# Batch 1 of a block-recurrent attention + ELU kernel: its turns taken from TensorE to VectorE and transfers, its state reading moved into its own first product

## The chip, the cores and the metric

The kernel runs on one core of one Trainium2 chip. The metric is device time in microseconds (us) for one execution. Below, PE is TensorE (matrix products), DVE is VectorE, ACT is ScalarE, POOL is GpSimd, and SP is the engine whose queue issues nearly all transfers.

## The reference

```python
B, H, S, Ns, D = 8, 8, 512, 32, 64             # x: (B,H,S,D), state: (B,H,Ns,D)
scale = 1.0 / np.sqrt(D)
scores = scale * np.matmul(x, state.transpose(0, 1, 3, 2))
a = np.exp(scores - scores.max(-1, keepdims=True))
a /= a.sum(-1, keepdims=True) + 1e-09
xread = np.matmul(a, state)                    # tokens read the state
scores2 = scale * np.matmul(state, x.transpose(0, 1, 3, 2))
a2 = np.exp(scores2 - scores2.max(-1, keepdims=True))
a2 /= a2.sum(-1, keepdims=True) + 1e-09
sread = np.matmul(a2, x)                       # the state reads the tokens
attn = np.concatenate([xread, sread], axis=2)
x = attn.transpose(0, 2, 1, 3).reshape(B * (S + Ns), H * D)
h = x @ w_in                                   # 512 -> 2048
g = np.where(h > 0.0, h, np.exp(np.minimum(h, 0.0)) - 1.0)
return (g @ w_out).astype(np.float32)          # 2048 -> 512
```

The weights come as 8-byte floats and are brought to 4 bytes in the kernel.

## The kernel before, in words

The work goes batch by batch over the eight batches, and the 256 state rows of all batches (what the state read) come last (`states`). For one batch there are these parts:

- **Attention.** `scores` multiplies the state with x, which has to stand with its features on the partitions, so x has to be *turned* first. There are two ways in the kernel. `turn_x` (L251) turns it on TensorE, 16 small products with the identity for each half of x, into PSUM, and `copy_x` (L260) copies it out with ScalarE. `load_blocks` (L141) and `turn_blocks` (L159) read x from memory in 16 transfers that already put the 32x32 blocks in place, and VectorE turns each block in itself, one instruction of 128x512 for a quarter of x. Then come the maxima, exponentials and sums (`column_max`, `column_exp`, `row_max`, `row_subtract` and so on), for two groups of heads g.
- **The state's reading.** `state_read` (L374) multiplies the column weights with x as loaded. For it the weights have to be turned: `turn_state` and `copy_state` (L347, L354) do it on TensorE and ScalarE, `move_state` (L359) with two block turns on VectorE and 16 transfers that put the blocks in place (`a_blocks` to `aT_s`). `keep_read` (L390) scales the result out of PSUM with ScalarE.
- **First product.** `make_m` (L418) multiplies the state into w_in, into a pair of PSUM banks, `copy_m` copies it to `m_sb`; `ffn1(b, fo)` (L453) makes one of 16 slices `fo` of the hidden layer from `m_sb` and the turned token weights `aT`. `exp_part` (ACT) and `max_part` (DVE) are the ELU and write `g_all`.
- **Second product.** In the first batch it is the plain one (`ffn2_row`, L480). From batch 1 on it is Strassen's scheme (class `Strassen`), partly in two levels (`Second`): its `sums()` (L589) are four VectorE instructions on `g_all`, two into `g_all` and two into `s`; its steps are seven products, the first in several pieces, and between the pieces the "hooks" of the next batch's attention run.

Batch 0, the batch in which all weights are also loaded and brought to 4 bytes, follows an order written out by hand: the string `plan` (L747). It also makes the attention of batch 1. In a step `name:numbers`, `w:n.1` and `w:n.2` are the two halves of bringing weight piece n to 4 bytes (ACT, DVE), `F`, `R`, `E`, `O` are the first product, exponential, maximum and output row of a slice, `M` and `Mc` make and copy m, `x` and `xc` are `turn_x` and `copy_x`, `sc` the scores, `mx tr ae sd tm ps te su pm tt` the steps of the softmax by group, `sT sTc sr src` turn, copy, reading and keeping of the state. Each `w:n.2` calls `fetch()`, which loads the next piece; when none is left it loads x of batch 1 and stores w_in for later.

The engines are wrapped in `InOrder` (L94): while `on` is set, each instruction is pinned behind everything that was traced before it on its engine. Otherwise a scheduler at compile time orders each engine's instructions by when its own model has them ready, earlier ones of the program first. TensorE and SP are pinned to the end. ScalarE and GpSimd are let go after the first batch, and VectorE in `batch(1)` (L864), and it stays so for the rest:

```python
        vector.on = False
        nxt = b + 1 < B
        hooks = attention(b + 1) if nxt else [turn_read]
```

In `batch(b)` (L847) the loop over `fo` makes the 16 slices. At `fo == 5` it calls `make_m` for the second half of w_in, in the last four slices it turns the blocks of the next batch, and in batch 1 every odd slice also makes a part of the weight sums (`weight_sum`) for Strassen's scheme, the last of them into `w_out`. After the loop come the sums and the steps. `hooks` holds for the next batch: scores to `move_state` behind the first piece, `state_read` and `keep_read` behind the seventh, then `load_x(b + 2)`, and in batch 1 the weights of `Second`.

Space: x as loaded (`x_sb`) has one buffer. The tiles of `tag="o"` (turned x, x in blocks, outputs) have two, those of `tag="w"` (weights as loaded, `xT_b`, `aT_s`, `a_blocks`, `t_w`, `s`) eleven. PSUM has eight banks; `pair(6)` is banks 6 and 7.

Of the kernel before, what the change touches and what calls it, by code (L numbers as in the profile page):

```python
# [25 lines left out]
def kernel(  # L26
# [106 lines left out]
    def load_x(b, engines):  # L133
        x_t[b] = xpool.tile([P, R, DM], FP32, name="x_sb")
        x_v = x[b].rearrange("h (p r) d -> p r h d", r=R)
        for r in range(R):
            engines[r % len(engines)].dma_start(
                out=x_t[b][:, r].rearrange("p (h d) -> p h d", d=D), in_=x_v[:, r]
            )
# [111 lines left out]
    def turn_x(b, i, first=6):  # L251

        ps = pair(first).rearrange("p t (j r q) -> p t j r q", j=2, q=64)
        for j in range(2):
            for r in range(R):
                m = 2 * i + j
                transpose(ps[:, :, j, r], x_t[b][:, r, m * P : (m + 1) * P])
        st[b, "xT", i] = ps
# [480 lines left out]
    def first_batch():  # L739

        plan = """  # L747
            kT kTc x:0.0 xc:0.0 x:0.1 w:0.1 xc:0.1 w:0.2 w:1.1 sc:0 Z:14 tr:0.0 tr:0.1 w:2.1 tm:0.0
            tm:0.1 ps:0.0 w:3.1 mx:0.1 mx:0.0 ps:0.1 w:1.2 ae:0.0 te:0.1 ae:0.1 sd:0.0 su:0.1 w:5.1
            M:0.0.0 sd:0.1 pm:0.1 w:3.2 Mc:0.0.0 te:0.0 sT:0 w:4.1 tt:0.1 su:0.0 sTc:0 w:5.2 pm:0.0  # L750
            w:8.1 Z:8 sr:0 tt:0.0 src:0 w:2.2 Z:14 F:0 w:6.1 F:1 w:8.2 R:0 M:0.0.1 R:1 E:0 Mc:0.0.1
            E:1 O:0 w:9.1 w:4.2 w:10.1 w:9.2 F:2 w:7.1 w:6.2 M:0.1.0 F:3 R:2 w:7.2 Mc:0.1.0 O:1
            w:11.1 E:2 R:3 w:10.2 M:0.1.1 w:12.1 F:4 w:11.2 Mc:0.1.1 O:2 R:4 E:3 w:14.1 w:12.2 F:5
            w:13.1 E:4 w:14.2 O:3 R:5 w:16.1 E:5 w:13.2 F:6 w:17.1 w:16.2 M:0.2.0 R:6 F:7 w:18.1
            w:17.2 O:4 Mc:0.2.0 w:18.2 w:20.1 kU w:15.1 E:6 O:5 w:20.2 w:21.1 w:15.2 w:19.1 F:8 kUc
            O:6 R:8 w:21.2 R:7 w:22.1 E:7 M:0.2.1 E:8 F:9 w:19.2 Mc:0.2.1 w:23.1 M:0.3.0 F:10 w:22.2
            w:24.1 O:7 w:23.2 R:9 Mc:0.3.0 E:9 w:25.1 w:24.2 M:0.3.1 F:11 Mc:0.3.1 R:10 w:25.2 O:8
            R:11 E:10 w:26.1 E:11 F:12 w:29.1 w:26.2 O:9 w:30.1 w:29.2 w:27.1 F:13 w:30.2 w:28.1
            O:10 w:27.2 R:13 R:12 w:28.2 x:1.0 w:31.1 O:11 E:12 E:13 xc:1.0 w:31.2 x:1.1 O:12 xc:1.1
            sc:1 O:13 mx:1.1 mx:1.0 ae:1.1 tr:1.0 ae:1.0 tr:1.1 sd:1.0 sT:1 tm:1.0 tm:1.1 ps:1.0  # L760
            F:14 sTc:1 sd:1.1 ps:1.1 te:1.0 sr:1 R:14 su:1.0 F:15 te:1.1 pm:1.0 E:14 src:1 su:1.1
            O:14 R:15 tt:1.0 pm:1.1 E:15 tt:1.1 M:1.0 O:15 Mc:1.0
        """.split()
        make_identity(nc, ident)
        o_ps = [bank(c) for c in range(R)]
        order = [lambda k=k: load_w_in(0, k) for k in range(4)]
        for c in range(1, FC + 1):
            if c < FC:
                order += [lambda c=c, k=k: load_w_in(c, k) for k in range(4)]
            order += [lambda fo=fo: load_w_out(fo) for fo in range(4 * c - 4, 4 * c)]  # L770
        w, h, e = [], {}, {}

        def fetch():
            if len(w) == 12 and len(raw_states) == 1:
                raw_states.append(load_states(1, B))
            if len(w) < len(order):
                w.append(order[len(w)]())
            elif 1 not in x_t:
                load_x(1, [sync])
                for c in range(FC):  # L780
                    k = slice(2 * c, 2 * c + 2)
                    sync.dma_start(out=w_in_mem[:, k], in_=w_in[:, k])

        raw_states = [load_states(0, 1, [sync, scalar])]
        load_x(0, [sync, scalar])
        for k in range(NRAW):
            fetch()
        groups = {
            "mx": column_max, "tr": turn_scores, "ae": column_exp, "tm": row_max,
            "ps": row_subtract, "te": row_exp, "su": row_sum, "pm": row_scale,  # L790
            "tt": turn_tokens, "sd": column_total,
        }
        whole = {
            "sc": scores, "sT": turn_state, "sTc": copy_state, "sr": state_read,
            "src": keep_read,
        }
        for step in plan:
            name, _, num = step.partition(":")
            num = [int(i) for i in num.split(".") if i]
            if name in ("kT", "kU"):  # L800
                turn_states(raw_states[name == "kU"], *((0, 1) if name == "kT" else (1, B)))
            elif name in ("kTc", "kUc"):
                copy_states(*((0, 1) if name == "kTc" else (1, B)))
            elif name == "Z":
                for i in range(num[0]):
                    matmul(bank(3)[:, :P], ident, ident, start=True, stop=True)
            elif name in groups:
                groups[name](*num)
            elif name in whole:
                whole[name](*num)  # L810
            elif name == "w":
                (convert_1, convert_2)[num[1] - 1](*w[num[0]])
                if num[1] == 2:
                    fetch()
            elif name == "F":
                h[num[0]] = ffn1(0, num[0])
            elif name == "R":
                e[num[0]] = exp_part(h[num[0]])
            elif name == "E":
                max_part(num[0], e[num[0]], h[num[0]])  # L820
            elif name == "O":
                ffn2_row(o_ps, num[0])
            elif name == "x":
                turn_x(*num)
            elif name == "M":
                make_m(*num)
                if len(num) == 2:
                    make_m(1, 1, first=4)
            elif name == "xc":
                copy_x(*num)  # L830
            else:
                assert name == "Mc", step
                if len(num) == 3:
                    copy_half(*num)
                else:
                    for g in range(G):
                        copy_m(*num, g, scalar.copy)
        for g in range(G):
            copy_m(1, 1, g, scalar.copy)

        for i in (1, 0):
            o_sb = opool.tile([P, 2, DM], FP32, tag="o", name="o_sb")
            for c in (1, 0):
                (scalar.copy, vector.tensor_copy)[c](out=o_sb[:, c], in_=o_ps[2 * i + c])
            store(0, i, o_sb)

    def batch(b):  # L847
        if b + 1 < B:
            load_blocks(b + 1)
        for fo in range(FO):  # L850
            elu(ffn1(b, fo), fo)
            if fo > 11 and b + 1 < B:
                turn_blocks(b + 1, fo - 12)
            if fo == FO // 4 + 1:
                for c in (2, 3):
                    make_m(b, c, first=6 if c == 2 else 0)
            if FO // 4 + 1 <= fo < FO // 4 + 5:
                c, g = divmod(fo - FO // 4 - 1, G)
                copy_m(b, 2 + c, g, vector.tensor_copy)
            if b == 1 and fo % 2 == 1:  # L860
                weight_sum((1, 2, 4, 3)[fo // 4], fo % 4 // 2)
            if b > 1 and fo == FO // 4 + 2:
                fetch_w_in(0, 0)
        vector.on = False  # L864
        nxt = b + 1 < B
        hooks = attention(b + 1) if nxt else [turn_read]
        if nxt and b > 0:
            s1 = hooks[0]
            hooks[0] = lambda: (s1(), fetch_w_in(2, 0))
        if b + 2 < B:  # L870
            hooks += [lambda: load_x(b + 2, [sync])]
        if b == 1:
            hooks += [lambda: second[4].weights(t_w[4]), lambda: second[3].weights(b22)]
            hooks += [lambda: second[5].weights(t_w[1]), lambda: second[7].weights(t_w[3])]
            used = {k: second[k] for k in (4, 3)}
        else:
            used = second
        whole = Strassen(2, used)
        whole.sums()
        for f in whole.steps():  # L880
            f()
            if hooks:
                hooks.pop(0)()
        if not nxt:
            fetch_w_in(2, 2)
        for i in (1, 0):
            store(b, i, whole.o_sb[i])
# [22 lines left out]
                )  # L910

    first_batch()
    load_x(2, [sync])
    for e in (scalar, gpsimd):
        e.on = False
    for b in range(1, B):
# [32 lines left out]
```

## Time and profile before

| | us |
|---|---|
| three runs | 746.68, 748.34, 748.26; median 748.26 |
| profiled execution, its own time | 746.17 |
| its span in the profile | 744.4 |

| place in the span | us |
|---|---|
| scores of batch 1 (TensorE) | 109.68 to 110.70 |
| first slice of batch 1 | from 128.72 |
| `make_m` of batch 1's second half | 139.11 to 140.99 |
| end of batch 1's first product | 159.29 |
| scores and `make_m` for batch 2 | 162.83 to 168.93 |
| reading of batch 2 | from 189.84 |

The granted TensorE clock is 1.0 throughout. In the lists of instructions the columns are start and length in us, engine, operation, what is written and read, and how many were put together in the row; in square brackets stands how long the engine was idle before, and what ended it. Products overlap on TensorE: the length of one row reaches into the next, so the price of a row is the step from its start to the start of the next one. The same holds for VectorE on a smaller scale. All instructions go through a wrapper, so all bear its line, L100, and are told apart by their tiles. A product of 4-byte floats is recorded as two.

### The profile page before, as it was taken

To read this page: it belongs to the slowest core of one execution; us is meant where nothing else is said; L and a number is where in the kernel's file an instruction comes from. 1 tells how busy PE (TensorE), PEld (TensorE's weight loads), DVE (VectorE), ACT (ScalarE), POOL (GpSimd) and SP (SyncE) were. 2 spreads that over 40 slices of the span, in tenths; PEclk is the share of its full clock that TensorE was granted. 3 is DMA by queue.
4 is the path that set the end of the run, shared out by engine and by line. 5 is a ranking of instruction groups with operands and counts; after the bars stand their busy time and mean duration, and the time that the engine had idled before them with its cause. 6 is when DMAs were issued, how large, how long until landed. Compare 5 with 4: busy or idle time off the path is not lost.

```text
span 744.4 us, 11377 instructions
## 1 busy us (share of the span) xinstructions
PE 723.7 (97%) x4472; PEld 502.5 (68%) x4472; DVE 486.0 (65%) x892; ACT 293.3 (39%) x539; POOL 34.4 (5%) x38
## 2 busy tenths in 40 slices
PE   4899999989999999999999999999999999999998
PEld 2544444348874798469944896479746894699886
DVE  2999975799437883677556864787367845556231
ACT  5899955542126311651055203621264106400420
POOL 0100002002000200010000200020002000000000
PEclk9999999999999999999999999999999999999999
DMA  9667900801634063503461164307340403003000
GB/s 282 225 201 239 326 0 1 167 4 22 177 94 133 5 179 84 160 1 106 122 153 46 26 173 110 116 13 187 83 144 1 143 33 137 1 1 142 29 4 25
DMA packets 126366, 76.25 MB, mean 102 GB/s; under 512 B 113768, under 2 KB 114280, under 8 KB 122472
## 3 DMA queue, kind: packets, MB, share of 16 engines
q1 hardware_dynamic: 124004, 74.90, 34.8%
q10 hardware_dynamic: 2308, 0.62, 0.4%
q8 instruction: 35, 0.57, 0.3%
q14 instruction: 19, 0.16, 0.1%
HBM read 59.24 MB, written 13.11 MB: 97 GB/s over the span
## 4 chain that ended last, share of the span: by engine, by line
PE 89%; DVE 6%; SPq 1%; DMA 1%; ACT 1%; issue 1%; POOL 0%; ACTq 0%; DVEq 0%; POOLq 0%
PE ps L100 89%; DVE w_in L100 2%; SPq L100 1%; DMA x_sb<-in_x_dram 1%; DVE g_all L100 1%; DVE total_t L100 0%; DVE s L100 0%; DVE top L100 0%; DVE w_out L100 0%; ACT e_sb L100 0%; POOL t_sb L100 0%; ACT xT L100 0%; DVE xT_b L100 0%; DVE aT L100 0%; DVE t_sb L100 0%
## 5 line engine op out<-in xcount | busy, mean ns | idle before, releaser
L100 PE MATMUL ps<-w_out,g_all 128*128 128x256 f32 (+2 forms) x1088 | 232.5, 366 | 1.1 <-DVE g_all L100 0.8
L100 PE MATMUL ps<-aT,m_sb 128*128 128x512 f32 x512 | 226.3, 595 | 1.1 <-DVE m_sb L100 0.8
L100 PEld LDWEIGHTS ps<-w_out,g_all 128*128 128x128 f32 x1088 | 176.6, 191 | 53.5 <-issue 37.1
L100 PEld LDWEIGHTS ps<-aT,m_sb 128*128 128x128 f32 x512 | 95.4, 190 | 122.0 <-issue 109.1
L100 ACT ACTIVATE e_sb<-ps 128x512 f32<-128x512 f32 (+1 forms) x144 | 82.5, 573 | 220.4 <-PE ps L100 205.1
L100 DVE SCALAR_TENSOR_TENSOR g_all<-e_sb,ps 128x512 f32<-128x512 f32 (+1 forms) x144 | 94.2, 656 | 101.0 <-ACT e_sb L100 100.4
L100 DVE TENSOR_TENSOR o_sb<-o_sb,ps 128x128 f32<-128x128 f32 (+2 forms) x170 | 52.6, 310 | 75.2 <-PE ps L100 73.5
L100 ACT ACTIVATE e_sb<-e_sb 128x512 f32<-128x512 f32 (+1 forms) x144 | 87.3, 606 | 4.6
L100 PE MATMUL ps<-t_w,s 128*128 128x256 f32 (+1 forms) x480 | 88.8, 339 | 0.0
L100 PEld LDWEIGHTS ps<-t_w,s 128*128 128x128 f32 x480 | 77.6, 191 | 8.1 <-DVE o_sb L100 0.2
L100 ACT COPY o_sb<-ps 128x512 f32<-128x512 f32 (+2 forms) x52 | 20.6, 424 | 151.7 <-PE ps L100 144.6
L100 ACT ACTIVATE raw<-raw 128x512 f32<-128x512 uint32 x64 | 43.7, 683 | 1.0
L100 DVE TENSOR_TENSOR s<-s,g_all 128x512 f32<-128x512 f32 (+1 forms) x36 | 32.2, 897 | 15.9 <-PE ps L100 15.5
L100 POOL TENSOR_TENSOR t_sb<-t_sb,top_t 128x512 f32<-128x512 f32 x16 | 16.7, 1047 | 517.0 <-DVE top_t L100 517.0
L100 DVE TENSOR_TENSOR g_all<-g_all,s 128x512 f32<-128x512 f32 (+1 forms) x36 | 32.1, 891 | 9.6 <-PE ps L100 9.6
L100 PE MATMUL ps<-w_in,kT 64*32 64x512 f32 (+1 forms) x576 | 34.0, 547 | 0.9 <-ACT a_s L100 0.9
L100 DVE TENSOR_TENSOR g_all<-g_all 128x512 f32<-128x512 f32 (+1 forms) x36 | 32.2, 894 | 0.5
L100 DVE TENSOR_TENSOR s<-g_all 128x512 f32<-128x512 f32 (+1 forms) x36 | 31.6, 883 | 0.8 <-DMA aT_s<-a_blocks 0.4
L100 PE MATMUL ps<-t_w,g_all 128*128 128x128 f32 (+1 forms) x240 | 32.1, 282 | 0.0
L100 PE MATMUL ps<-w_in,s 128*128 128x128 f32 x240 | 31.2, 277 | 0.0
L100 PEld LDWEIGHTS ps<-t_w,g_all 128*128 128x128 f32 x240 | 29.8, 192 | 0.5
L100 PEld LDWEIGHTS ps<-w_in,s 128*128 128x128 f32 x240 | 28.7, 192 | 0.6 <-DVE o_sb L100 0.5
(86 smaller groups left out, 557.1 us busy)
## 6 DMA issues: line engine op xcount, KB each, us to landing
w_in<-w_in_mem SPq DMA_DIRECT2D x26, 1024.0 KB, 5.9
raw<-in_moe_w_in_dram SPq DMA_DIRECT2D x16, 512.0 KB, 4.6
raw<-in_moe_w_out_dram SPq DMA_DIRECT2D x16, 512.0 KB, 4.5
out_dram<-o_sb SPq DMA_DIRECT2D x16, 512.0 KB, 2.8
x_sb<-in_x_dram SPq DMA_DIRECT2D x30, 256.0 KB, 4.9
x_blocks<-in_x_dram SPq DMA_DIRECT2D x96, 64.0 KB, 2.4
w_in_mem<-w_in SPq DMA_DIRECT2D x4, 1024.0 KB, 8.3
aT_s<-a_blocks SPq DMA_DIRECT2D x96, 32.0 KB, 1.9
```

What stands on the lines that cost most here:

```text
L100: ins = getattr(self.engine, name)(*args, **kw)
```

## The change

In `plan`, the steps `x xc` and `sT sTc sr src` of batch 1 are taken out. In place of the first come four `bt` (`turn_blocks`), in place of the second comes `ab` (`move_state`), on VectorE between the row sum and the maximum of slice 14. `fetch()` loads x in blocks ahead of x as it is. The reading of batch 1 is made at `fo == 5` of `batch(1)`, and the load of batch 2's x, which needs x's one buffer, moves behind it. The two pairs of banks of `make_m` there are exchanged for batch 1. And VectorE is let go behind `whole.sums()` rather than ahead of the hooks, so that the four sums of batch 1 stay in the order of the program.

```diff
--- before.py
+++ after.py
@@ -756,9 +756,9 @@
             O:6 R:8 w:21.2 R:7 w:22.1 E:7 M:0.2.1 E:8 F:9 w:19.2 Mc:0.2.1 w:23.1 M:0.3.0 F:10 w:22.2
             w:24.1 O:7 w:23.2 R:9 Mc:0.3.0 E:9 w:25.1 w:24.2 M:0.3.1 F:11 Mc:0.3.1 R:10 w:25.2 O:8
             R:11 E:10 w:26.1 E:11 F:12 w:29.1 w:26.2 O:9 w:30.1 w:29.2 w:27.1 F:13 w:30.2 w:28.1
-            O:10 w:27.2 R:13 R:12 w:28.2 x:1.0 w:31.1 O:11 E:12 E:13 xc:1.0 w:31.2 x:1.1 O:12 xc:1.1
-            sc:1 O:13 mx:1.1 mx:1.0 ae:1.1 tr:1.0 ae:1.0 tr:1.1 sd:1.0 sT:1 tm:1.0 tm:1.1 ps:1.0
-            F:14 sTc:1 sd:1.1 ps:1.1 te:1.0 sr:1 R:14 su:1.0 F:15 te:1.1 pm:1.0 E:14 src:1 su:1.1
+            O:10 w:27.2 R:13 R:12 w:28.2 w:31.1 bt:1.0 bt:1.1 O:11 E:12 bt:1.2 E:13 bt:1.3 w:31.2 O:12
+            sc:1 O:13 mx:1.1 mx:1.0 ae:1.1 tr:1.0 ae:1.0 tr:1.1 sd:1.0 tm:1.0 tm:1.1 ps:1.0
+            F:14 sd:1.1 ps:1.1 te:1.0 R:14 su:1.0 ab:1 F:15 te:1.1 pm:1.0 E:14 su:1.1
             O:14 R:15 tt:1.0 pm:1.1 E:15 tt:1.1 M:1.0 O:15 Mc:1.0
         """.split()
         make_identity(nc, ident)
@@ -776,6 +776,7 @@
             if len(w) < len(order):
                 w.append(order[len(w)]())
             elif 1 not in x_t:
+                load_blocks(1)
                 load_x(1, [sync])
                 for c in range(FC):
                     k = slice(2 * c, 2 * c + 2)
@@ -822,6 +823,10 @@
                 ffn2_row(o_ps, num[0])
             elif name == "x":
                 turn_x(*num)
+            elif name == "bt":
+                turn_blocks(*num)
+            elif name == "ab":
+                move_state(*num)
             elif name == "M":
                 make_m(*num)
                 if len(num) == 2:
@@ -852,8 +857,12 @@
             if fo > 11 and b + 1 < B:
                 turn_blocks(b + 1, fo - 12)
             if fo == FO // 4 + 1:
+                if b == 1:
+                    state_read(1)
+                    keep_read(1)
+                    load_x(2, [sync])
                 for c in (2, 3):
-                    make_m(b, c, first=6 if c == 2 else 0)
+                    make_m(b, c, first=0 if (c == 2) == (b == 1) else 6)
             if FO // 4 + 1 <= fo < FO // 4 + 5:
                 c, g = divmod(fo - FO // 4 - 1, G)
                 copy_m(b, 2 + c, g, vector.tensor_copy)
@@ -861,7 +870,6 @@
                 weight_sum((1, 2, 4, 3)[fo // 4], fo % 4 // 2)
             if b > 1 and fo == FO // 4 + 2:
                 fetch_w_in(0, 0)
-        vector.on = False
         nxt = b + 1 < B
         hooks = attention(b + 1) if nxt else [turn_read]
         if nxt and b > 0:
@@ -877,6 +885,7 @@
             used = second
         whole = Strassen(2, used)
         whole.sums()
+        vector.on = False
         for f in whole.steps():
             f()
             if hooks:
@@ -910,7 +919,6 @@
                 )
 
     first_batch()
-    load_x(2, [sync])
     for e in (scalar, gpsimd):
         e.on = False
     for b in range(1, B):
```

## The prediction

> **What bounds the kernel now.** I read the page first, then TensorE's waits over the whole span, then the instructions in order of time around each place that the diff touches.
>
> ```profile
> PE 723.7 (97%) x4472; PEld 502.5 (68%) x4472; DVE 486.0 (65%) x892; ACT 293.3 (39%) x539; POOL 34.4 (5%) x38
> ```
>
> TensorE is busy for 723.7 of 744.4 us, so an edit is worth what it takes off TensorE's own stream, or off one of its waits. The waits (us in total, times, longest) from 37 to 200 us:
>
> ```profile
> PE ps L100 <- DVE xT_b L100: 2.3, 1, 2.3
> PE ps L100 <- DVE g_all L100: 0.8, 1, 0.8
> PE ps L100 <- DVE m_sb L100: 0.8, 1, 0.8
> ```
>
> After 200 us there is one of 0.3 us. So two waits can be won in batch 1 (for xT_b at 163.9, for m_sb at 145.5; the one for g_all is at 37 us and is not touched). Next TensorE's rows at the end of the first batch (start, us, instructions):
>
> ```profile
> 97.60 3.60 PE L100 MATMUL ps<-w_out,g_all 128*128 128x512 f32 x8
> 101.13 0.71 PE L100 MATMUL ps<-ident,x_sb 64*128 64x64 f32 x16
> 101.77 3.70 PE L100 MATMUL ps<-w_out,g_all 128*128 128x512 f32 x8
> ...
> 109.68 1.09 PE L100 MATMUL ps<-xT,kT 64*32 64x512 f32 x16
> 110.70 3.70 PE L100 MATMUL ps<-w_out,g_all 128*128 128x512 f32 x8
> 114.24 1.04 PE L100 MATMUL ps<-ident,a_s 128*128 128x128 f32 x8
> 115.11 1.88 PE L100 MATMUL ps<-aT,m_sb 128*128 128x512 f32 x4
> 116.92 1.10 PE L100 MATMUL ps<-x_sb,aT_s 128*32 128x64 f32 x64
> ```
>
> The step from start to start is the price of a group. These rows are packed, so each is on the path: 0.64 us for a turn of x (two of them), 0.87 for the turn of the weights, 1.03 for the reading. Then VectorE at the end of batch 1:
>
> ```profile
> 160.91 0.65 DVE L100 SCALAR_TENSOR_TENSOR g_all<-e_sb,ps 128x512 f32<-128x512 f32 x1
> 161.48 1.21 DVE L100 TENSOR_TENSOR g_all<-g_all 128x1024 f32<-128x1024 f32 x1
> 162.61 2.35 DVE L100 TENSOR_TENSOR s<-g_all 128x1024 f32<-128x1024 f32 x2
> 164.87 0.68 DVE L100 TENSOR_TENSOR t<-t_w,t 128x512 f32<-128x512 f32 x1
> 165.47 0.70 DVE L100 STREAM_TRANSPOSE xT_b<-x_blocks 128x512 f32<-128x512 f32 x1
> 166.10 1.18 DVE L100 TENSOR_TENSOR w_out<-w_out 128x1024 f32<-128x1024 f32 x1
> 167.31 0.69 DVE L100 TENSOR_REDUCE top<-ps 128x1 f32<-128x512 f32 x1
> ```
>
> The sums (g_all, s) ran ahead of the fourth turned block, for which the scores of batch 2 wait. And what that batch's reading waits for:
>
> ```profile
> 177.12 10.43 SPq L100 DMA_DIRECT2D aT_s<-a_blocks  x16
> ...
> 189.46 0.69 DVE L100 TENSOR_TENSOR s<-g_all 128x512 f32<-128x512 f32 x1 [0.45 <-DMA aT_s<-a_blocks]
> 189.84 1.10 PE L100 MATMUL ps<-x_sb,aT_s 128*32 128x64 f32 x64
> ```
>
> The last transfer of the weights lands at about 189.4, and the reading starts at 189.84: 0.3 us of slack, no more.
>
> **First batch, up to the scores.** Gone are 2 x 0.64 = 1.28 us of TensorE. From 97.60 to the end of the scores now takes 13.10 us; without the turns it is three groups of 8 products at 3.46 (24 of them took 10.39 in batch 1, 128.72 to 139.11), 0.15 for the change of tile shape before the scores, and the scores' 1.02: 11.55. I take 1.5 off, so the scores end at 109.2. The four block turns cost VectorE 0.63 each from start to start. It is in order there: the step before ends at 101.92, four turns and the two maxima (1.2) bring the last turn to 105.64, and TensorE wants it at 108.1. VectorE's idle 4.04 us ahead of the column maximum cover them; the weight steps after (2.36) end at 108.0, the two loose subtractions of 0.70 (b) at 109.4, and the maximum can start at 109.2 + 0.25. It just fits; without that cover up to 1.4 us would be late. ScalarE loses 2 x 1.06 of copies, off the path.
>
> The 16 block transfers (0.64 each to issue, median of that row, 2.4 to land) go first on SP's queue at 75.9, where x was loaded. They land by about 89 and are wanted at 101.9. Behind them x and the four stores of w_in move by some 10 us; x is now wanted 30 us later, w_in is overwritten at 142.8. Both hidden.
>
> **First batch, from the scores to the next output row.** From the scores' end to the row at 119.78 is 9.08 us, and TensorE filled it with 3.54 (output row), 0.87 (turn), 1.81, 1.03 (reading), 1.83. Without turn and reading it has 7.0. But that row waits for a maximum (g_all), and VectorE's chain to it gets longer: the row exponential ends at 116.87, that is 6.2 after the scores, as before (it waits for GpSimd, not for what goes). The row sum ends VectorE's next three steps at 7.3, and now the two turns of the weights stand there, 2 x 0.63, so the maximum runs from 8.6 to 9.25 and the row starts at 9.3 (before: maximum done at 119.0, 8.3 after, with 0.8 of slack). So the 1.9 us taken off TensorE become 2.3 us of waiting, and the stretch is 0.2 longer. The row starts at 118.5 in place of 119.78: **-1.3**. The next output step has its maximum about 1 us before TensorE gets to it, as now. ScalarE's two copies of the weights (1.07) go, off the path. The 16 transfers of the weights take SP from 117.9 to 128.3 and land at about 130.2; batch 1 reads them at about 137.8. The stores of the first output come at 128.4, right behind.
>
> [...] The row: eight turns of 128x128 took TensorE 0.87 us, 0.11 each. [...]
>
> **Batch 1, middle.** The reading's 1.03 us comes back here, on TensorE's path. Behind it the first product of make_m goes to banks 0 and 1 (0.95 us), the second waits until ScalarE has kept the reading (0.76 for the two copies, after one e_sb pair): 0.1 late, bounds 0 and 1 us (ScalarE's row of 1.25 us for the pair in between). **+1.15**. VectorE gets 1.1 us more ahead of the m_sb copy that TensorE waited 0.76 for; the loose subtractions into w_in (2.1 us) that made it late can still stand in front of the maximum, so I leave 0.2 of the wait: **-0.55**, bounds 0 and -0.76. load_x(2), 4 issues, moves behind the 16 block loads on SP: the blocks come some 4 us earlier, x lands near 150 and is read near 187.
>
> **Batch 1, end.** This is where a large gain seems to lie. In order, the fourth block is turned right after the last maximum, so the scores need not wait: from 162.83 to 168.93 is 6.10 us, and batch 2's same two rows (scores and make_m, 246.94 to 249.67) take 2.73: 3.4 us off TensorE. But the reading of batch 2 hangs on another chain: column maximum, weights, their turns, 16 issues at 0.65, landing. It took from 167.31 to 189.46, 22.15 us, and in batch 2 from 248.14 to about 270.3, the same. So only the start of the column maximum counts. Before, it is 6.40 after the last maximum's start (160.91). After: maximum 0.57, turn 0.63, w_out 1.21, two g_all sums of 1.13 (one of them had run at 146.17, between products, and is now pinned behind everything), two s sums 2.26: 6.93. The sums go first, since they are earlier in the program and ready. So the landing comes 0.55 later, the slack takes 0.3: **+0.2**, and TensorE's 3.4 us turn into a wait of about 3.5 in front of the reading. Bounds: -3.4 (the chain no longer binds) to +2.8 (see below). Nothing else in the pinned stretch is late: the s sums are wanted after three pieces of 3.45, some 11 us on.
>
> Batches 2 to 7 keep their code, since VectorE is never put back in order.
>
> **Sum:** -1.3 + 1.15 - 0.55 + 0.2 = -0.5 us against the profiled execution's 746.17 (span 744.4 and 1.8 around it). The median of the three runs is 2.1 above that, so 748.26 - 0.5 = 747.8.
>
> **Rivals.** (1) *The wait at the end of batch 1 is really won*: the column maximum runs ahead of the sums, and the landing follows the scores. For it: it is ready at about 164, four us before the sums end; the sums are not wanted for 11 us. Against: VectorE's rows of before show the s sums taken as soon as they can be. Then +0.2 becomes -3.4: 748.26 - 4.1 = 744.2. (2) *Slower: the weights of batch 2 land later still.* The place is VectorE between the last maximum and the column maximum. What ran in its gaps before (the subtractions into w_in, 2.1, and into t, 0.68) can fall in there, since the removed early sum and the moved reading shift those gaps. There is no slack, so each us is a us of TensorE; all 2.8 give -0.5 + 2.8 = +2.3, 750.6. It decides when the column maximum starts later than some 9.6 us after the last maximum. (3) *Sums pinned in vain*: the fourth block is late for another reason (its transfers), TensorE still waits for it and the reading does not: 748.3, no change.
>
> **Numbers.** A difference of 0.3% (2.2 us) is about what a measurement can tell from none. My forecast and its near variants (from -2.2 to +2.2, rival 3 in it) get 0.55, rival 1 with the partial gains beyond -2.2 gets 0.27, rival 2 and other losses 0.18. The range goes from rival 1 to rival 2, 744.2 to 750.5, and leaves out about 2 in 10.
>
> **What would show it.** Right: no turns by TensorE ahead of the scores at the first batch's end; a wait of TensorE for g_all of about 2.3 us near 116; none for xT_b near 163; one for the transfers of aT_s of about 3.5 us ahead of the reading near 186 to 189; the wait for m_sb below 0.4. Wrong: no wait before that reading (rival 1), or a column maximum over 9 us behind the last maximum (rival 2), or waits in batches 2 to 7 that were not there.

## The result, and the profile after

The changed kernel takes 748.5 us (median of six runs, 746.89 to 749.67), the kernel before 748.3 (six runs, 746.68 to 748.55). The ratio is 1.0005, with a 95% interval of 0.9988 to 1.0023: no difference that can be measured. The forecast was 747.8, in effect no change, as the prediction takes 0.3% for about what a measurement can tell from none. The profiled execution took 748.85 us with a span of 747.0, against 746.17 and 744.4 before, so in the two profiles the change looks 2.6 us slower, where the forecast was 0.5 faster.

In the page, the line of busy times answers to the one shown of before:

```profile
PE 725.2 (97%) x4432; PEld 504.5 (68%) x4432; DVE 489.1 (65%) x898; ACT 290.5 (39%) x533; POOL 34.4 (5%) x38
```

TensorE has 40 instructions fewer (the turns of x and of the weights), and yet 1.5 us more of busy time. Its waits from 30 to 200 us:

```profile
PE ps L100 <- DMA aT_s<-a_blocks: 2.3, 1, 2.3
PE ps L100 <- DVE g_all L100: 2.0, 1, 2.0
```

Both waits of batch 1, for xT_b (2.3) and for m_sb (0.8), are gone, and two have come that are longer together (4.3 against 3.1): one for a maximum at the end of the first batch, one for the transfers of the weights ahead of the reading of batch 2. TensorE's rows around them (start, us, instructions, idle time before and its releaser):

```profile
98.44 10.46 PE L100 MATMUL ps<-w_out,g_all 128*128 128x512 f32 x24
108.83 1.09 PE L100 MATMUL ps<-xT_b,kT 64*32 64x512 f32 x16
109.85 3.70 PE L100 MATMUL ps<-w_out,g_all 128*128 128x512 f32 x8
113.39 3.60 PE L100 MATMUL ps<-aT,m_sb 128*128 128x512 f32 x8
118.96 5.40 PE L100 MATMUL ps<-w_out,g_all 128*128 128x512 f32 x8 [1.97 <-DVE g_all L100]
124.28 1.95 PE L100 MATMUL ps<-w_in,kT 64*32 64x512 f32 x32
...
140.09 1.10 PE L100 MATMUL ps<-x_sb,aT_s 128*32 128x64 f32 x64
141.12 1.95 PE L100 MATMUL ps<-w_in,kT 64*32 64x512 f32 x32
143.00 17.80 PE L100 MATMUL ps<-aT,m_sb 128*128 128x512 f32 x40
160.63 3.62 PE L100 MATMUL ps<-w_out,g_all 128*128 128x256 f32 x16
164.18 1.09 PE L100 MATMUL ps<-xT_b,kT 64*32 64x512 f32 x16
...
187.84 0.63 PE L100 MATMUL ps<-x_sb,aT_s 128*32 128x64 f32 x6
190.81 1.05 PE L100 MATMUL ps<-x_sb,aT_s 128*32 128x64 f32 x58 [2.34 <-DMA aT_s<-a_blocks]
```

Two things are to be seen. The turns are gone ahead of the scores (108.83), and the scores of batch 2 (164.18) follow without a gap. And the output row at 118.96, eight products like those that take 3.5 us in the rows around it, takes 5.32 to the start of the next row. The table by windows says why (core; the window, busy time and count of PE, PEld, DVE, ACT and POOL, then the granted clock, the DMA share and GB/s):

```profile
120.00:122.00 2.00, 2.00 (x4) 0.79 (x3) 1.84 (x3) 0.00 (x0) 1.05 (x1) 0.58 0.30 49
122.00:124.00 2.00, 2.00 (x4) 0.68 (x2) 0.00 (x0) 0.00 (x0) 0.00 (x0) 0.57 0.30 49
192.00:194.00 2.00, 2.00 (x6) 1.53 (x6) 0.97 (x2) 0.21 (x1) 0.00 (x0) 0.50 0.99 401
```

and of before, over the first and the last of these windows:

```profile
120.00:122.00 2.00, 2.00 (x6) 0.84 (x5) 1.41 (x4) 1.20 (x2) 1.05 (x1) 1.00 0.00 0
...
192.00:194.00 2.00, 2.00 (x11) 1.75 (x10) 0.69 (x1) 0.00 (x0) 0.00 (x0) 1.00 1.02 414
```

Behind each of the two new waits the granted clock fell to half: 0.50 for 3.41 us in the trace's clock record, about 1.7 us of lost work each. A third such fall stands at 24.7 to 28.1 us, where the diff changes nothing. Before's profiled execution has none. The two executions, step by step (us, with the forecast):

| stretch | before | after | step | forecast |
|---|---|---|---|---|
| up to the row at 97.60 | 97.60 | 98.44 | +0.84 | 0 |
| to the scores' end | 110.70 | 109.85 | -1.69 | -1.5 |
| to the row of slice 14 | 119.78 | 118.96 | +0.03 | +0.2 |
| that row | 123.30 | 124.28 | **+1.80** | 0 |
| to the reading of batch 1, before `make_m` | 139.11 | 140.09 | 0 | 0 |
| to the end of `make_m` | 140.99 | 143.00 | +1.03 | +1.15 |
| to the end of batch 1's first product | 159.29 | 160.63 | -0.67 | -0.55 |
| to the end of batch 2's reading | 190.88 | 191.79 | -0.43 | +0.2 |
| to the end of the span | 744.4 | 747.0 | **+1.7** | 0 |

The edits' own steps add up to -1.7. The two falls of the clock behind waits give back 3.5. The first step, +0.84, is not the price of the fall at 24 us: 0.31 of it is there before that fall (the row at 24.29 in before starts at 24.60 in after) and 0.38 behind it (37.05 and 37.43), since before's TensorE waits there for other engines anyhow (0.34 and 0.79 us). "Two queues" below, with no fall, comes to this row only at 98.69. Where the 0.84 comes from stays open.

### The profile page after: what moved, and what is told of

Its sections match the earlier page's. It is cut to its first block, busy times and chain, and to the rows that moved or that the text cites. A ratio compares the mean times of both kernels' runs of the same rounds, so it can differ in the third digit from the quotient of the medians.

```text
span 747.0 us, 11349 instructions
## 1 busy us (share of the span) xinstructions
PE 725.2 (97%) x4432; PEld 504.5 (68%) x4432; DVE 489.1 (65%) x898; ACT 290.5 (39%) x533; POOL 34.4 (5%) x38
## 4 chain that ended last, share of the span: by engine, by line
PE 80%; DVE 12%; SPq 3%; ACT 2%; DMA 1%; issue 1%; POOL 0%; ACTq 0%; DVEq 0%; POOLq 0%
PE ps L100 80%; DVE w_in L100 3%; SPq L100 3%; DVE w_out L100 3%; DVE g_all L100 2%; DMA x_sb<-in_x_dram 1%; DVE top L100 1%; DVE t_sb L100 1%; DVE top_t L100 1%; DVE s L100 1%; DVE total_t L100 1%; DMA aT_s<-a_blocks 1%; ACT e_sb L100 0%; DVE a_blocks L100 0%; POOL t_sb L100 0%
## 5 line engine op out<-in xcount | busy, mean ns | idle before, releaser
L100 PE MATMUL ps<-w_out,g_all 128*128 128x256 f32 (+2 forms) x1088 | 235.6, 370 | 2.4 <-DVE g_all L100 2.0
L100 PEld LDWEIGHTS ps<-w_out,g_all 128*128 128x128 f32 x1088 | 178.6, 193 | 57.4 <-issue 37.2
```

The source lines that it names most:

```text
L100: ins = getattr(self.engine, name)(*args, **kw)
```

## The experiments

My theory at this point: the edits win about 1.7 us of TensorE's stream, and new waits, by the slower clock that may follow them, give it back. Its parts are tried one by one: the order of VectorE alone and undone, each wait shortened, the waits filled with products, and x's turns alone. Each kernel was compared with before on the same chip, so the ratios are set side by side, and where I say "against after" it is a difference of two ratios, good to about 0.2% (1.6 us).

### The order alone

```diff
 (kernel before)
-        vector.on = False
         nxt = b + 1 < B
...
         whole.sums()
+        vector.on = False
```

> The kernel before with one part alone: VectorE is let go behind the four sums. Theory (the wait is handed on): in the compiled order four loose subtractions now stand between the last maximum and the fourth turned block, since its transfers are still behind the load of x; the wait of TensorE for xT_b shrinks from 2.3 to about 1 us, but the column maximum starts about 9.3 us after the last maximum's start (6.4 before), so the reading of batch 2 waits some 2.5 us for aT_s: 2.5 to 4.3 us slower than before, the upper end when TensorE's clock falls behind that wait as it did in the changed kernel. Rival (the wait at the scores is really won by the order): 2 us or more faster than before, no wait for aT_s.

Measured: 750.73 us against 747.88, ratio 1.0039 (1.0025 to 1.0052). VectorE's rows:

```profile
161.23 0.65 DVE L100 SCALAR_TENSOR_TENSOR g_all<-e_sb,ps 128x512 f32<-128x512 f32 x1
...
164.20 0.71 DVE L100 STREAM_TRANSPOSE xT_b<-x_blocks 128x512 f32<-128x512 f32 x1
...
170.46 0.69 DVE L100 TENSOR_REDUCE top<-ps 128x1 f32<-128x512 f32 x1
```

and TensorE's waits in batch 1:

```profile
PE ps L100 <- DMA aT_s<-a_blocks: 3.0, 2, 2.3
PE ps L100 <- DVE xT_b L100: 0.8, 1, 0.8
...
PE ps L100 <- DVE m_sb L100: 0.8, 1, 0.8
```

Pinning takes only 1.5 of the 2.3 us off the wait for xT_b, since what is pinned ahead of the fourth block comes before it. The column maximum starts 9.2 us after the last maximum instead of 6.4, as four subtractions of the weight sums now stand between the last maximum and the fourth block (161.80 to 164.20), and the reading's wait is 3.0. From the end of batch 1's first product to the end of the reading it takes 33.70 us, against 31.59 in before: 2.1 of the 2.9 us. That is rival 2's mechanism, in this kernel and not in the changed one: the part of the change that looks like its largest gain costs 2.9 us by itself.

### The order undone in the changed kernel

```diff
 (kernel after)
+        vector.on = False
         nxt = b + 1 < B
...
         whole.sums()
-        vector.on = False
```

> The changed kernel with one part undone: VectorE is let go ahead of the hooks, as before. Theory: the fourth block is turned in time all the same, since its transfers no longer stand behind the load of x; one of the sums runs early again, the column maximum starts 5.8 us after the last maximum's start (6.84 in the changed kernel), and the wait for aT_s is 1.1 us shorter (about 1.2): 1.1 us faster than the changed kernel, up to 2.8 if the clock no longer falls behind it. Rival (the order is what keeps the block ahead of the sums): the wait for xT_b of some 2 us comes back and the time is the same or longer.

Measured: 744.67 us against 747.88, ratio 0.9964 (0.9951 to 0.9977), 0.41% or 3.1 us below after. TensorE's waits from 40 to 200 us, and VectorE's rows at the end of batch 1:

```profile
PE ps L100 <- DVE g_all L100: 2.0, 1, 2.0
PE ps L100 <- DMA aT_s<-a_blocks: 1.4, 1, 1.4
```

```profile
161.94 0.65 DVE L100 SCALAR_TENSOR_TENSOR g_all<-e_sb,ps 128x512 f32<-128x512 f32 x1
162.51 0.69 DVE L100 STREAM_TRANSPOSE xT_b<-x_blocks 128x512 f32<-128x512 f32 x1
...
167.63 0.69 DVE L100 TENSOR_REDUCE top<-ps 128x1 f32<-128x512 f32 x1
```

The wait for xT_b doesn't come back. VectorE turns the fourth block at 162.51, right behind the last maximum (161.94), with no pin on it. What put it in time is then not the order of VectorE but another edit. The likeliest is the load of batch 2's x, which stood ahead of the 16 block loads on SP's queue and now stands behind them (issued from 145.22 in after, the blocks from 133.41); that edit wasn't tried by itself. It can't be that the blocks arrive too late at run time: in before their last issue ends at 148.19, and a block load takes 2.4 us to land, well ahead of the first turn at 156.25. If this edit acts, it does so through the order that the scheduler's model chooses, and no run here shows that. The pin only adds to the chain: without it the column maximum starts 5.7 us after the last maximum, against 6.8, and the wait ahead of the reading is 0.9 shorter. The rest of the 3.1 us goes with the clock ("The runs by their clock").

### The weights' turns later in the first batch

```diff
 (kernel after)
-            F:14 sd:1.1 ps:1.1 te:1.0 R:14 su:1.0 ab:1 F:15 te:1.1 pm:1.0 E:14 su:1.1
+            F:14 sd:1.1 ps:1.1 te:1.0 R:14 su:1.0 F:15 te:1.1 pm:1.0 E:14 ab:1 su:1.1
```

> The changed kernel with the two turns of the weights on VectorE behind the maximum of slice 14 rather than ahead of it. Theory: TensorE's wait for g_all at 117 to 119 us falls from 2.0 to about 0.8 (the row sum's chain remains), and if that is too short for the clock to fall, the following row takes 3.5 us rather than 5.3: 1.2 to 3.0 us faster than the changed kernel. Rival (the wait is the exponential's and GpSimd's alone): it stays at 2.0.

Measured: 745.33 us against 747.88, ratio 0.9963 (0.9949 to 0.9976), 3.1 us below after. TensorE's rows at that place:

```profile
117.05 3.70 PE L100 MATMUL ps<-w_out,g_all 128*128 128x512 f32 x8 [0.89 <-DVE g_all L100]
120.68 1.95 PE L100 MATMUL ps<-w_in,kT 64*32 64x512 f32 x32
```

The wait is 0.89 where it was 1.97, and the row takes 3.63. A wait that is 1.1 shorter can't give 3.1 us by itself. What stays: the wait of 2.33 for aT_s, behind which this profile shows the full clock. So a wait of that length doesn't always bring a fall; "The runs by their clock" shows when it did.

### The weights of batch 2 through two queues

```diff
 (kernel after, in move_state)
-                sync.dma_start(
+                engine = scalar if b == 2 and q % 2 else sync
+                engine.dma_start(
```

> The changed kernel with the 16 transfers of batch 2's turned weights issued half by SP, half by ScalarE. Theory (the issues one after the other are what the reading waits for): the last issue comes 5 us earlier, the wait of 2.3 us for aT_s is gone, and with it the slow clock behind it: 2.3 to 4.0 us faster than the changed kernel. Rival (VectorE's chain or the transfers themselves end last, or ScalarE's issues start late): a wait of 1 us or more stays.

Measured: 743.2 us against 747.88, ratio 0.9934 (0.9922 to 0.9947), 5.3 us below after. The issues on SP and on ScalarE's queue:

```profile
177.52 5.21 SPq L100 DMA_DIRECT2D aT_s<-a_blocks  x8
```

```profile
177.49 5.57 ACTq L100 DMA_DIRECT2D aT_s<-a_blocks  x8
```

and TensorE at the reading:

```profile
182.84 3.62 PE L100 MATMUL ps<-w_out,g_all 128*128 128x256 f32 x16
186.39 1.10 PE L100 MATMUL ps<-x_sb,aT_s 128*32 128x64 f32 x64
```

The 16 issues in a row were 10.4 us of the chain that ended last. In two rows of eight they are 5.2 and 5.6, and the reading runs without a wait. The wait of 2.0 for g_all is still there, this time at the full clock.

### The waits filled with products

```diff
 (kernel after)
+    def fill(n):
+        for i in range(n):
+            matmul(bank(7)[:, :P], ident, ident, start=True, stop=True)
...
-        return [..., lambda: (state_read(b), keep_read(b))]
+        return [..., lambda: (fill(10 if b == 2 else 0), state_read(b), keep_read(b))]
...
-            F:14 sd:1.1 ps:1.1 te:1.0 R:14 su:1.0 ab:1 F:15 te:1.1 pm:1.0 E:14 su:1.1
+            F:14 sd:1.1 ps:1.1 te:1.0 R:14 su:1.0 ab:1 F:15 Y:8 te:1.1 pm:1.0 E:14 su:1.1
...
+            elif name == "Y":
+                fill(num[0])
```

The last entry of that list is the hook behind the seventh product. The 18 products of the identity with itself write results that nobody reads; nothing else is changed.

> The changed kernel with products of the identity with itself, which nothing reads, put on TensorE in its two waits: 8 ahead of the output row of slice 14 (about 1.9 us of the 2.0), 10 ahead of the reading of batch 2 (about 2.4 us of the 2.3 to 2.9). What TensorE waits for stays as it is. Theory (each wait makes the clock fall in part of the runs, 3.41 us at half speed, 1.7 us each): the mean clock over the runs rises from 0.995 to 0.998 or more, as before the change, and the time is 1.5 to 3 us shorter than the changed kernel's 748.5, though work was added. Rival (the falls have nothing to do with the waits): the same clock and 748.5 to 749.

Measured: 745.13 us against 748.49, ratio 0.9964 (0.9952 to 0.9976), 3.1 us below after, with work added. TensorE's rows at the first wait and at the second:

```profile
116.17 1.95 PE L100 MATMUL ps<-ident 128*128 128x128 f32 x16
118.31 3.70 PE L100 MATMUL ps<-w_out,g_all 128*128 128x512 f32 x8 [0.18 <-DVE g_all L100]
...
185.40 2.40 PE L100 MATMUL ps<-ident 128*128 128x128 f32 x20
188.47 1.05 PE L100 MATMUL ps<-x_sb,aT_s 128*32 128x64 f32 x58 [0.44 <-DMA aT_s<-a_blocks]
```

What TensorE waited for comes no earlier by these products: from the scores' end (109.20) to the output row it is 9.11 us, as in after, and from the end of batch 1's first product (158.29) to the second part of the reading 30.18, as in after. Only its idle time is gone, and with it the loss: the output row takes 3.63 and not 5.32 us, and the mean granted clock over the runs is 0.9987 (11 runs), where after's is 0.9948 (6 runs). The difference of 0.0039, times a span of 747, is an estimated 2.9 us, about the 3.1 measured. This is the run that separates the wait from what comes behind it.

### The chain first, the sums later

```diff
 (kernel after)
+        vector.on = False
         nxt = b + 1 < B
...
-        whole.sums()
-        vector.on = False
+        whole.sums(later=b == 1)
+        if b == 1:
+            first = hooks[0]
+
+            def chain_first():
+                first()
+                vector.on = True
+                whole.second_sums()
+                vector.on = False
+
+            hooks[0] = chain_first
```

With `later` set, `sums()` makes only the two sums into `g_all`, and `second_sums()` makes the two into `s`. `first` is the hook that goes from the scores to `move_state` of batch 2.

> The changed kernel with the two s sums behind batch 2's softmax and turns on VectorE, pinned there, and VectorE let go ahead of the g_all sums. Theory (the start of the column maximum sets the end of batch 1): it starts some 4.1 us after the last maximum's start (6.84 in the changed kernel), the wait for aT_s (2.3) is gone or below 0.3, but the s sums end about 17 us after the last maximum while TensorE wants the first at 15: a wait of about 1 us for s takes its place. 1.3 to 3.0 us faster than the changed kernel. Rival (the transfers set the reading's wait whatever starts them): 2 us of wait for aT_s stay, and 1 us is added.

Measured: 745.77 us against 748.49, ratio 0.9967 (0.9954 to 0.998), 2.8 us below after. TensorE's waits from 40 to 200 us, and VectorE's rows of the last maximum and of the column maximum:

```profile
PE ps L100 <- DVE g_all L100: 2.0, 1, 2.0
PE ps L100 <- DVE s L100: 1.5, 1, 1.5
```

```profile
162.20 0.65 DVE L100 SCALAR_TENSOR_TENSOR g_all<-e_sb,ps 128x512 f32<-128x512 f32 x1
...
166.23 0.69 DVE L100 TENSOR_REDUCE top<-ps 128x1 f32<-128x512 f32 x1
```

This is rival 1 made on purpose. The column maximum starts 4.0 us after the last maximum (162.20 to 166.23) and the wait for aT_s is gone, but the products that use s wait 1.5, as the first of the two sums into s now ends only at about 179. From the end of batch 1's first product to the end of the reading (160.58 to 190.56) it takes 29.98 us, against 31.16 in after and 31.59 in before. So even this order of VectorE wins only 1.2 us beside after and 1.6 beside before.

### x's turns alone

```diff
 (kernel before)
-            O:10 w:27.2 R:13 R:12 w:28.2 x:1.0 w:31.1 O:11 E:12 E:13 xc:1.0 w:31.2 x:1.1 O:12 xc:1.1
+            O:10 w:27.2 R:13 R:12 w:28.2 w:31.1 bt:1.0 bt:1.1 O:11 E:12 bt:1.2 E:13 bt:1.3 w:31.2 O:12
...
+                load_blocks(1)
                 load_x(1, [sync])
...
+            elif name == "bt":
+                turn_blocks(*num)
```

> The kernel before with one part alone: x of batch 1 turned in blocks by VectorE; the turn and the reading of its weights stay on TensorE in the first batch, and nothing else is changed. Theory (TensorE's products are what bounds this stretch, and VectorE's gap ahead of the column maximum covers the turns): from the output row at 97.6 to the scores' end 1.5 to 1.7 us shorter, the waits for xT_b and m_sb in batch 1 as before: 1.6 us faster than before, 746.3 beside 747.9. Rival (VectorE is late for the column maximum): the gain is below 0.5.

Measured: 746.59 us against 748.49, ratio 0.998 (0.9964 to 0.9995), a gain of 1.5 by the ratio and 1.9 by the medians. TensorE's rows:

```profile
97.65 10.46 PE L100 MATMUL ps<-w_out,g_all 128*128 128x512 f32 x24
108.04 1.09 PE L100 MATMUL ps<-xT_b,kT 64*32 64x512 f32 x16
109.06 3.70 PE L100 MATMUL ps<-w_out,g_all 128*128 128x512 f32 x8
```

From 97.65 to the scores' end it is 11.41 us, against 13.10 before: 1.69, the same as in after. The 32 turns were worth 0.053 us each. This part of the change does what it says and brings no wait of TensorE into the first batch or batch 1 (behind them there is one of 1.0 us for o_sb, at 272.6; before's only one for o_sb was 0.3); its 1.69 is about as much as all the edits together win (1.7). Before's wait for xT_b is still there, and in this execution the clock falls behind it:

```profile
164.60 0.62 PE L100 MATMUL ps<-xT_b,kT 64*32 64x512 f32 x2 [2.33 <-DVE xT_b L100]
...
165.06 4.00 PE L100 MATMUL ps<-w_in,kT 64*32 64x512 f32 x26
```

The same 26 instructions took 2.30 in before, from 166.70.

### Three of these edits together

The changed kernel with the edits of "The weights' turns later", "The order undone" and "The weights of batch 2 through two queues".

> The changed kernel with three edits: the weights' turns behind the maximum of slice 14, VectorE let go ahead of the hooks, and batch 2's weight transfers issued from two queues. Theory: of TensorE's waits after the first 40 us only about 0.9 for g_all is left; clock at 0.998 or above; 741 to 742.5, that is 0.8 to 0.9% faster than the kernel before. Rival (what is taken away there comes back in batch 2 or behind): 743 or more, with a new wait after 190 us.

Measured: 741.85 us against 748.49, ratio 0.992 (0.9903 to 0.9937): the fastest of all, 0.8% below before. TensorE's waits after 40 us:

```profile
PE ps L100 <- DVE g_all L100: 0.9, 1, 0.9
PE ps L100 <- DVE o_sb L100: 0.8, 2, 0.6
```

The mean clock is 0.9987. The rival's new wait behind 190 us is there, but small: the longer of the two for o_sb, 0.6, ends at 267.6; before's only one for o_sb was 0.3.

### The runs by their clock

Each run has its own mean clock. In "The order alone" (12 runs) the times go with it in steps: 748.3 us at 1.000 (2 runs), 750.2 at 0.998 (4), 751.5 at 0.995 (3), 752.0 at 0.993 (3). One fall is 3.41 us at half clock, 1.7 us of 747 or 0.0023 of the mean, so these are none, one, two and three falls. The steps are not always that clear: before's nine runs at 0.998 in the second group lie between 746.62 and 749.50. What a fall cost depended on where it came: behind the wait for g_all 1.8 us, at 24 us under 0.1 (from the row ahead of it to the row behind it 12.83 us in after, 24.60 to 37.43, and 12.76 in before, 24.29 to 37.05). So a difference of mean clocks, times the span, is an estimate. Runs at 1.000 have no fall in them and compare what the instructions and waits themselves cost (before was run in two groups, beside the first four and beside the last four experiments):

| kernel | median at clock 1.000 (runs) | mean clock over all its runs |
|---|---|---|
| before, first and second group of runs | 746.4 (4), 746.6 (5) | 0.9976, 0.9972 |
| after | none of 6 | 0.9948 |
| order alone | 748.3 (2) | 0.9963 |
| order undone | 743.6 (5) | 0.9978 |
| weights' turns later | 743.9 (2) | 0.9972 |
| two queues | 743.0 (2) | 0.9990 |
| waits filled | 744.6 (5) | 0.9987 |
| chain first | 743.5 (1) | 0.9961 |
| x's turns alone | 744.8 (2) | 0.9979 |
| all three | 741.4 (3) | 0.9987 |

"Waits filled" is after's stream with its waits as long as they were: 744.6, 2.0 below before, beside the -1.7 of the steps (with 18 products added). None of after's own six runs had the clock full throughout. Its mean clock is 0.0028 below before's of the first group; 0.0028 x 747 = 2.1 us. So -1.7 + 2.1 = +0.4, and 0.05% (0.4 us) was measured; six runs are few for so close an agreement.

The same sum can be made for each edit of the changed kernel. The step is read from the profiles, over the stretch that the edit touches (scores' end to the row of slice 14, or end of batch 1's first product to the end of batch 2's reading); the clock's part is the difference from after's mean clock, times 747:

| against after, us | step | clock | sum | measured |
|---|---|---|---|---|
| order undone | -1.22 | -2.24 | -3.5 | -3.1 |
| weights' turns later | -1.09 | -1.79 | -2.9 | -3.1 |
| two queues | -2.93 | -3.14 | -6.1 | -5.3 |
| waits filled | 0.01 | -2.91 | -2.9 | -3.1 |
| chain first | -1.18 | -0.97 | -2.2 | -2.8 |
| all three | -4.01 | -2.91 | -6.9 | -6.4 |

All agree within the 1.6 us to which such a difference is known. Without the clock's part every sum would be short, by 1.6 to 3.1 us.

**When a wait brought a fall.** In the clock record of all ten traces, the stretches of time from one change of the clock to the next are whole multiples of 3.413 us (in after 6.827, 92.160 and 68.267), and each fall lasts 3.413 (only at the very end of the record are they cut short). So the changes lie on a grid, and each trace can be cut into its windows of 3.41 us. The grid stands differently to the start of the kernel in each execution. Some of the windows, with the time that TensorE was idle in them by its rows:

| execution, window | idle in it, us | clock in the next window |
|---|---|---|
| before, 162.09 to 165.50 (first part of the wait for xT_b) | 1.60 | 1.00 |
| before, 165.50 to 168.91 (the rest of that wait) | 0.73 | 1.00 |
| x's turns alone, 162.11 to 165.52 (all of the same wait) | 2.33 | 0.50 |
| after, 116.89 to 120.30 (all of the wait for g_all) | 1.97 | 0.50 |
| two queues, 115.45 to 118.86 (most of the same wait) | 1.63 | 1.00 |
| after, 188.57 to 191.98 (nearly all of the wait for aT_s) | 2.24 | 0.50 |
| weights' turns later, 182.34 to 185.75 and 185.75 to 189.16 (the same wait in two parts) | 0.94, 1.45 | 1.00, 1.00 |
| after, 21.32 to 24.73 (two waits, of 0.57 and 1.47) | 2.04 | 0.50 |
| before, 18.73 to 22.14 and 22.14 to 25.55 (the same two waits and a shorter one) | 0.91, 1.46 | 1.00, 1.00 |

Of the some 2100 windows of the ten traces, from the first at full clock on, eleven are followed by a fall. In those TensorE was idle for 1.97 us or more (nine within the kernel, with 1.97 to 2.35, and two at its end, with 2.05 and 3.36), in all the others for 1.63 or less. So the same wait brought a fall in one execution (2.33 in one window) and none in another (1.60 and 0.73 in two) by where the edges of the grid cut it, and two waits that were each shorter than any that brought one alone (0.57 and 1.47) brought one together.

## Why the prediction was right, and where it was not

**The forecast** (no change, 0.7 us off the median) held, but partly by luck: -0.5 was forecast as a sum of small terms, and the true sum is -1.7 from the edits and about +2.1 from the clock. The second term stood nowhere in the prediction.

**First batch.** -1.3 forecast, -1.66 measured. The turns' price was right to 0.2: 1.5 was taken off, where the rows' starts alone (0.64 per 16) gave 1.28, and 1.69 was measured, in "x's turns alone" as well. No run shows the 0.15 us that the forecast's sum has for the change of tile shape: the 24 products take 10.39 us up to the scores' start (98.44 to 108.83 in after), what the sum has for them without it. VectorE's idle time did cover the four turns: the column maximum starts 0.18 us behind the scores' end (110.03 and 109.85), in before 0.25. The wait for g_all, 2.3 forecast, is 1.97 (and 0.89 where the weights' turns stand one step later). Most of that difference is a slip in a sum: 9.08 less 0.87 and 1.03 is 7.18, not 7.0. The place and the cause were right; the price was not, as I counted only its length.

**Batch 1, middle.** +1.15 forecast, +1.03 measured: the exchange of the banks costs nothing. Of the wait for m_sb I had left 0.2; all of it went (-0.67 against -0.55).

**Batch 1, end.** The reading, not the scores, sets the time here: shown by "two queues", where the reading's chain is cut and the gain appears, and by "order alone", where it is made longer and the kernel slows. VectorE's rows of the last maximum and of the column maximum in after:

```profile
162.34 0.65 DVE L100 SCALAR_TENSOR_TENSOR g_all<-e_sb,ps 128x512 f32<-128x512 f32 x1
...
169.18 0.68 DVE L100 TENSOR_REDUCE top<-ps 128x1 f32<-128x512 f32 x1
```

They are 6.84 us apart; 6.93 was forecast. From the column maximum's start to the reading it is 21.63 us in after (169.18 to 190.81), 21.66 in "order alone" and 21.65 in "order undone", where I had taken 22.15 from before's 189.46. That is the term that was off here, by 0.5: the step came out -0.43 and not +0.2. The wait came out 2.34 and not 3.5 for this and because the first six instructions of the reading ran ahead of it (187.84 to 188.47). And the cause that I gave for the fourth block (that VectorE is in order) is not the one that acts: "order undone" shows it in time without the order.

**The rivals.** Rival 1 didn't happen, and "chain first" shows that it could have given 1.6 us and not 3.4, since the sums are then late. I had put them as "not wanted for 11 us", which doesn't hold once the whole chain goes first. Rival 2's mechanism is real, at 9.2 us in "order alone", but in the changed kernel no loose subtraction stands between the last maximum and the column maximum (the one into t ran at 158.23). Rival 3 (pinned in vain) fell, as no wait for xT_b remained.

**The step that was missing.** In both places I let products turn into a wait ("2.3 us of waiting", "a wait of about 3.5") and priced the wait at its length alone. The waits of TensorE had a second price here, the slower clock that followed some of them (0.50 for 3.41 us, 1.7 to 1.8 us lost); "waits filled" shows it apart from the wait itself (3.1 us below after, though what TensorE waited for came no earlier). Before pays it too, with one such wait, for xT_b ("x's turns alone" has the fall behind it). The change took that one away and made two, and the mean clocks, 0.9976 and 0.9948, differ by about one fall a run. Nothing of it was in before's profiled run: its 2.3 us wait at 163.9 was cut by an edge of the grid and had the full clock behind it. But before's three times, 746.68 beside 748.26 and 748.34, are 1.6 apart, about one fall, and could have raised the question.

## What to carry to other kernels

This kernel is bound by TensorE (busy for 97% of the span). Products taken out of its stream were worth about their step from start to start (x's 32 turns: 1.28 us by the rows' starts, 1.69 measured), and the wait for g_all that took the place of 1.9 us of them (0.87 and 1.03) lasted 1.97 and lost, in after's profiled execution, another 1.8 by the clock. See what ends last before you shorten anything, and look at the granted clock behind each wait, in more than one execution. Here no fall came behind a window of the grid (3.41 us) in which TensorE was idle for 1.63 us or less, and a wait made shorter than that won more than the time cut off it ("The weights' turns later": 3.1 us for 1.1). If the wait must stay, shorten the chain (here 16 transfers issued on one queue, split over two: 5.3 us below after) or let TensorE do something harmless in it (3.1 below after). And take a change of several parts apart: here x's turns alone won 1.5 to 1.9 us, and the new order of VectorE, which seemed the largest gain, was a loss both alone (2.9 us) and with the rest (3.1).

## What the runs showed of the hardware

- Waits of TensorE of 1.97 to 2.34 us led to 3.41 us at half clock in some executions and to none in others, at the same place: behind the wait for g_all of 2.0, the row takes 5.32 or 5.33 to the start of the next in after, "order undone" and "chain first", and 3.63 in "two queues"; the wait for aT_s of 2.3 has a fall behind it in after and none in "weights' turns later". A fall cost 1.7 to 1.8 us where TensorE had no other wait to absorb it, and under 0.1 at 24 us, where before's TensorE waits for 0.34 and 0.79 us and after's doesn't.
- In these ten traces the clock changed only on a grid of 3.413 us, and fell for one step of it when TensorE was idle for 1.97 us or more of the step before (eleven cases); with 1.63 us or less it never fell. No window lies between these two. One wait of 1.97 was enough, and so were two of 0.57 and 1.47 in one window (after, 21.32 to 24.73).
- What makes the clock fall no run here shows beyond that; the figures are TensorE's idle time by its rows.
- A row of issues on one queue was a price by itself: 16 transfers of this kind took 0.65 us each to issue, 10.4 in all. Eight of them on each of two queues took 5.2 on SP's, 0.65 each as before, and 5.6 on ScalarE's, 0.70 each; whether ScalarE's queue would be faster alone no run shows.
- Left open: how many of after's falls over its six runs stand behind the two waits and how many at 24 us (only one execution has a trace), and what lies between 1.63 and 1.97 us of idle time.
